# A 50-point transform in column halves of the TensorE array, with the work's order laid out anew

## The chip, the core and the metric

The kernel runs on one core of a Trainium2 chip. The metric is the device time of one launch in microseconds (us). The engines named below are TensorE (PE, with its weight loads shown apart as PEld), VectorE (DVE), ScalarE (ACT), GpSimd (POOL) and SyncE (SP), which here issues nearly all DMAs.

## What is computed

Eight sequences of 3200 positions with 256 channels go through a filter in the frequency domain and then a gated convolution. Cut to what matters:

```python
X = np.fft.rfft(x, axis=1)                      # x: (8, 3200, 256)
Yr = Xr @ w_r - Xi @ w_i + b_r                  # 256 x 256 weights
Yi = Xr @ w_i + Xi @ w_r + b_i
Y  = soft_threshold(Yr, 0.01) + 1j * soft_threshold(Yi, 0.01)
x  = np.fft.irfft(Y, n=3200, axis=1)

gate_pre = sum(conv_w[k] * shifted(x, k) for k in range(5))   # causal, per channel
out = (sigmoid(gate_pre) * (x @ w_val)) @ w_out
```

All of it is fp32 in and out.

## The kernel before

**The transforms.** 3200 is taken as 64 x 50 (N1 = 64, N2 = 50), so each transform is two short ones done as matrix products with constant matrices, once forth and once back. A batch (one of the eight sequences) goes through these steps, with the names of the trace:

- p1 (lines 553 to 560, tile p): the forward 50-point transform from x, 8 pieces a batch, on quarters of the array (64 x 64, with 50 rows used). The result is folded into s and stored to a_dram.
- s2 (line 631, tile s; line 623 for the last group): the forward 64-point transform on 64 x 64 quarters, 6 pairs of pieces and one whole-array piece a batch.
- mix_sum and mix (lines 749 and 745, tile y_ps; 735 and 736 for the last group): the products with the complex weights over the whole array. Operands are split into a high and a low part in the fp32r format, and three products of parts stand for one. The bias is seeded by line 727, the threshold is lines 757 and 759.
- s1i (line 700, tile z_ps; line 694 for the last group): the 64-point transform back, on 64 x 64 quarters. ACT copies it out (line 710), SP stores it to z_dram.
- s2i (line 810, tile y_p): the 50-point transform back. It is in `positions`, called 8 times a batch (k from 0 to 7). A z load (line 800) brings 100 rows (Q = 2 x 50) by 4 x 256 channels into zl. For each channel half c and each of 4 positions m, one fp32 product takes 100 rows by 128 channels of zl as weights and streams 100 columns of the constant g2; the result lies on 128 partitions, one per channel, and is copied by ACT to y_sb (line 814; for k = 0 lines 818 to 822).
- gated (lines 847 to 911): the value product v (line 844, tile v_ps), the convolution (lines 871 and 874, tile acc, on ACT and DVE), sigmoid (884), gate (886), the split of the gated values (348 and 350) and the projection o (line 844, tile o_ps). For the last batches v and o use unsplit fp32 weights (line 840, w_late). ACT copies o out (line 911) and SP stores it.

The forward part of one batch is interleaved with the back part of the batch before.

**What sets the order.** The order on every engine is fixed when the program is built, by the class `Plan`. `add(at, engine, busy, fn, ...)` gives a piece a due time `at`, an engine, an assumed duration `busy` in ns, what it uses and sets, and the buffers that it opens. `order` then simulates the engines: at each step it takes, among the pieces of one engine that could start within SLACK (20 ns; 50 on SP) of the earliest one, the piece with the lowest due time. The due unit is such that a batch has 13 (T = 13). The dictionary O holds the offsets of the due times ("load_z", "y", "conv" and so on), and two entries for PE's mode. The assumed durations are not those of the trace: s2i is planned at 1500 ns.

Each PE piece has a mode: "q" for pieces on quarters of the array, "f" for fp32 and "r" for fp32r on the whole array. SWITCH (line 239) adds about 100 ns for a passing into "q" or out of it, and nothing between "f" and "r". In the choice of the next piece (lines 191 to 193) a "q" piece gets its due time lowered by O["together"] while PE is in mode "q"; when PE is in another mode and only one "q" piece could start, its due time is raised by O["hold"]:

```python
lone = e == "PE" and sum(c[1]["mode"] == "q" for c in near) < 2
start, p = min(near, key=lambda c: (c[1]["at"] + (0.0 if e != "PE" or c[1]["mode"] != "q" else -O["together"] if mode == "q"
                                                   else O["hold"] if lone else 0.0), c[0]))
```

The buffers count too: SLOTS gives three buffers of two PSUM banks with the tag ps_2, which p1, s2, s1i, s2i, v and o share, two for y_ps, and three for zl.

Of the kernel before, what the change touches and what calls it, by code (L numbers as in the profile page):

```python
# [18 lines left out]
P = 128  # L19
HP = P // 2  # L20
# [4 lines left out]
Q = NH * N2  # L25
# [79 lines left out]
class Plan:  # L105
# [11 lines left out]
    def add(self, at, engine, busy, fn, uses=(), sets=(), new=None, delay=None, mode="r", kb=0, chain=None, extra=0):  # L117
        n = len(self.pieces)
        before = set()
        for key in uses:  # L120
            before |= set(self.writers.get(key, ()))
        for key in sets:
            before |= set(self.readers.get(key, ())) | set(self.writers.get(key, ()))
        for key in uses:
            self.readers.setdefault(key, []).append(n)
        for key in sets:
            self.writers[key], self.readers[key] = [n], []
        p = dict(n=n, at=at, engine=engine, busy=busy, fn=fn, before=before, new=new or {}, mode=mode, kb=kb, extra=extra,
                 tiles={key[:2] for key in (*uses, *sets)}, delay=busy + LAND[engine] if delay is None else delay)
        p["behind"] = {self.last[chain]} if chain in self.last else set()  # L130
        if chain:
            self.last[chain] = n
        self.pieces.append(p)
        return n

    def order(self):
# [41 lines left out]
        while len(done) < len(pieces):  # L178
            best = None
            for e in engines:  # L180
# [5 lines left out]
                if not could:  # L186
# [4 lines left out]
# [3 lines that stand above are left out]
                if best is None or start < best[0]:  # L194
# [56 lines left out]
def act(n, kind="copy"):  # L251
    return {"copy": 45, "cast": 95, "mul": 104, "conv": 187, "relu": 198, "sigmoid": 103}[kind] + n / 1.2
# [5 lines left out]
NW = (NT - 1) * N1 + P  # L258
NG = NT // 2 * P + P
T = float(NU)  # L260
O = {'spread': -31.571,
     'hold': 1.3548,
     'together': 0.9587,
     'later': 40.4566,
     'load_x': -3.5845,
     'p1': -4.4613,
     'p1_step': 1.7844,
     'load_a': -4.8762,
     's2': -1.2484,
     's1i': 0.7694,  # L270
     'p3': 3.4728,
     'load_z': -14.7609,
     'y': 13.0605,
     'conv': 13.0179,
     'val': 2.3373,
     'gate': -21.6564,
     'project': 4.8084,
     'late_val': 6.023,
     'late_out': 14.484,
     'turn': -25.2941,  # L280
     'pre': 0.9193,
     'mix_sum': -2.2347,
     'p1_1': -2.3762,
     'load_x_1': 3.5351,
     'p1_2': 0.8883,
     'p3_0': 0.312}
WARM = 2, 1, 1, 1, 8
SLOTS = {"x": 3, "zl": 3, "y_hl": 2, "s1": 2, "a": 2, "xs": 2, "sx": 1, "xz": 1, "tp": 3, "zst": 2,
         "acc": 2, "g_hl": 2, "o": 2, "ps_y": 2, "ps_2": 3, "a_dram": 2, "z_dram": 2}
# [6 lines left out]
def fourier_filter_then_gated_conv(ctx: ExitStack, tc: tile.TileContext, x, w_r, w_i, b_r, b_i,  # L296
                                   w_val, conv_w, w_out, f1, f2, g1, g2, out):
    nc = tc.nc
# [3 lines left out]
    dram = ctx.enter_context(tc.tile_pool(name="dram", bufs=2, space=bass.MemoryType.DRAM))  # L302
    LATE_VAL, LATE_OUT = set(LATE[int(O["late_val"]):]), set(LATE[int(O["late_out"]):])
    plan = Plan(SLOTS)
    add = plan.add
# [21 lines left out]
    def buffer(key, tag, shape, dtype=F32):  # L327
        pool = ps if tag.startswith("ps_") else dram if tag.endswith("_dram") else sb
        tl[key] = pool.tile(shape, dtype, name=key[0], tag=tag, bufs=SLOTS[tag])
        return tl[key]  # L330
# [7 lines left out]
    def two_banks(key, tag="ps_2"):  # L338
        return buffer(key, tag, [P, 2, 512])

    def split(at, n, key, src, high, low, uses=(), new=None, first=None):

        hl = key + ("high",), key + ("low",)

        def cast():
            if first:
                first()
            nc.scalar.copy(out=high(), in_=src())
        add(at, "ACT", act(n, "cast"), cast, uses, [hl[0]], new, chain=key[0])
        add(at + 0.001, "DVE", dve(n), lambda: nc.vector.tensor_tensor(out=low(), in0=src(), in1=f32(high()), op=ALU.subtract),  # L350
            [*uses, hl[0]], [hl[1]])
        return hl
# [26 lines left out]
    def from_float64(at, n, views, uses, done, new=None, first=None):  # L379
# [34 lines left out]
        for k, (fn, busy) in enumerate(steps):  # L414
            def piece(k=k, fn=fn):
                if k == 0 and first:
                    first()
                fn()
            add(at + O["later"] + O["spread"] * k, "DVE", busy, piece, uses, done, new if k == 0 else None, delay=busy + (130 if k == 12 else 0))

    def load_matrix64(at, name, w, dst, uses=()):
# [9 lines left out]
        def views():  # L431
# [4 lines left out]
                     lambda: [buffer(key, "zl", [P, MB * D]) for key in keys[1:]])  # L436
        split(at + O["later"] + O["spread"] * 13 + 0.02, n, ("w", name), lambda: tl[keys[1]][:, n:2 * n].rearrange("p (j d) -> p j d", j=2),
              lambda: dst[:, 0], lambda: dst[:, 1], [keys[1] + (0,)])
# [84 lines left out]
    def p1(b, u, at):  # L523
# [8 lines left out]
        def load(h):  # L532
            xt = room(kx, x_tag, 4 * D) if h in (0, None) else tl[kx]
            src = x[b].rearrange("(n m) c -> n (m c)", m=N1)
            for g in range(NH) if h is None else (h,):
                eng = QUEUES[g][1] if early else nc.sync
                lo = (N1 - 3 - 4 * u if g else 4 * u) * D
                n = 3 * D if g and u == 0 else 4 * D
                by_rows(eng, xt[half(g), 0:n], src[:, lo:lo + n], rows)
                if n < 4 * D:  # L540
                    by_rows(eng, xt[half(g), n:], src[:, NM * D:(NM + 1) * D], rows)
# [3 lines left out]
        else:  # L545
            add(at + O["load_x"] + O["load_x_1"] * (b == 1), "SP", 700, lambda: load(None), STORED if b == 1 else (),
                [kx + (0,), kx + (1,)], {kx: x_tag}, kb=400, chain="x")
# [245 lines left out]
    def positions(b, k, at):  # L793

        bk = (b, k)
        kz, kp = ("zl", bk), ("y_p", bk)

        def load():
            zt = buffer(kz, "zl", [P, MB * D])
            nc.sync.dma_start(out=zt[0:Q], in_=tl["z_dram", b][:, k * MB * D:(k + 1) * MB * D])  # L800
        add(at + O["load_z"], "SP", 400, load, [("z_dram", b, u) for u in range(NU)], [kz + (0,)], {kz: "zl"}, kb=400, chain="zl")

        def s2i():
            zt = tl[kz].rearrange("p (m c) -> p m c", m=MB)
            p = two_banks(kp)
            for c in range(2):
                for m in range(MB):
                    g = g2_sb[0:Q, 0:Q] if k == m == 0 else g2_sb[0:Q, Q:2 * Q]
                    dst = p[:, c, 0:TB].rearrange("p (g n) -> p g n", n=N2)[:, m:2 * MB - m:2 * MB - 1 - 2 * m, :]
                    nc.tensor.matmul(dst, zt[0:Q, m, c * P:(c + 1) * P], g, start=True, stop=True)  # L810
        add(at, "PE", 1500, s2i, [kz + (0,), ("g2", 0, 0)], [kp + (0,)], {kp: "ps_2"}, mode="f", chain="s2i")
        up = (H0 + MB * k) * N2
        if k:
            add(at + 0.1, "ACT", act(2 * TB), lambda: nc.scalar.copy(  # L814
                out=pair(y_sb, up, (N1 - MB + 1 - 2 * MB * k) * N2, MB * N2), in_=tl[kp][:, :, 0:TB].rearrange("p c (h n) -> p c h n", h=2)),
                [kp + (0,)], [("y", "up", k), ("y", "down", k)])
        else:
            add(at + 0.1, "ACT", act(TB), lambda: nc.scalar.copy(out=y_sb[:, :, up:up + MB * N2], in_=tl[kp][:, :, 0:MB * N2]),
                [kp + (0,)], [("y", "up", 0)])
            add(at + 0.1, "ACT", act(2 * (MB - 1) * N2), lambda: nc.scalar.copy(  # L820
                out=y_sb[:, :, (H0 + N1 - MB + 1) * N2:], in_=tl[kp][:, :, MB * N2:(2 * MB - 1) * N2]), [kp + (0,)], [("y", "down", 0)])
            add(at + 0.1, "ACT", act(2 * N2), lambda: nc.scalar.copy(out=mid_sb[:, b % 2], in_=tl[kp][:, :, (2 * MB - 1) * N2:TB]),
                [kp + (0,)], [("mid", b % 2, 0)])
        if k == 1:
            def turned():
                old = y_sb[:, :, N1 * N2:].rearrange("p c (m n) -> p c m n", n=N2)
                new = y_sb[:, :, 0:H0 * N2].rearrange("p c (m n) -> p c m n", n=N2)
                nc.vector.tensor_copy(out=new[:, :, :, 1:], in_=old[:, :, :, :N2 - 1])
            add(at + 0.1, "DVE", 283, turned, [("y", "down", 0), ("y", "down", 1)], [("y", "back", 0)])
        if k == NB - 1:  # L830
            mid = (H0 + NM) * N2
            add(at + 0.1, "ACT", act(2 * N2), lambda: nc.scalar.copy(out=y_sb[:, :, mid:mid + N2], in_=mid_sb[:, b % 2]),
                [("mid", b % 2, 0)], [("y", "mid", 0)])
# [138 lines left out]
    for b in range(B):  # L972
# [12 lines left out]
        start = (b + 1) * T + O["p3"] + O.get(f"p3_{b}", 0.0)  # L985
# [31 lines left out]
```

## Time and profile before

| | us |
|---|---|
| median of 3 runs | 877.88 (877.44 to 878.52) |
| the profiled execution | 876.76 |
| its span, first to last instruction | 875.0 |

The page gives the busy share of each engine over the span, then the chain of work that ended last, then groups of instructions by source line with their mean duration. A duration of one matmul in such a group runs from its start to its modelled end, and the matmuls overlap; so the time that a piece takes on PE is read from the distance of its start to the start of the next piece, in the chain in order of time. "x16" behind a line is the number of instructions merged there; an fp32 product is two instructions. In the table of windows each row is a stretch of the span with the busy time of PE, PEld, DVE, ACT and POOL, the clock that TensorE was granted, the DMA share and GB/s.

### The profile page before, as it was taken

The numbers are of one execution on the slowest core, as the hardware profiler recorded it, in microseconds if no ns is written. First come the engines' busy times: TensorE is split into PE (matmuls) and PEld (weight loads), VectorE is DVE, ScalarE is ACT, GpSimd is POOL, SyncE is SP. The second block draws the span as 40 slices with busy tenths as digits, with TensorE's granted clock in tenths as the row PEclk, the third lists the DMA queues.
The fourth block names the chain that finished last, engine by engine and source line by source line (L and its number), as shares of the span: only waits on it lengthen the run. The fifth ranks groups of instructions, "written<-read, shape, count | busy, mean of one in ns | idle before, by whom it ended". The sixth has DMA issues, their size and how long they took to land.

```text
span 875.0 us, 21750 instructions
## 1 busy us (share of the span) xinstructions
PE 841.8 (96%) x8790; PEld 726.1 (83%) x8790; DVE 767.1 (88%) x1262; ACT 617.9 (71%) x1030; POOL 3.7 (0%) x11
## 2 busy tenths in 40 slices
PE   8987987999999999999999999999999999999997
PEld 2355665988899989999999989989999999998874
DVE  2435598899999999999999999999999999899896
ACT  1323555787777786878878786878868787786663
POOL 0000000000000000000000000000010000000000
PEclk9967999999999999999999999999999999999999
DMA  6679777658774758747674767657674466415412
GB/s 169 184 186 234 222 197 230 220 175 257 224 214 153 222 158 247 235 149 204 216 239 146 224 173 253 217 157 210 212 216 136 133 166 179 123 64 168 150 60 92
DMA packets 123966, 162.13 MB, mean 185 GB/s; under 512 B 10592, under 2 KB 98298, under 8 KB 123866
## 3 DMA queue, kind: packets, MB, share of 16 engines
q1 hardware_dynamic: 122106, 157.47, 60.1%
q10 hardware_dynamic: 1760, 3.28, 1.4%
q8 instruction: 69, 1.13, 0.6%
q14 instruction: 31, 0.25, 0.1%
HBM read 82.06 MB, written 78.64 MB: 184 GB/s over the span
## 4 chain that ended last, share of the span: by engine, by line
PE 79%; DVE 9%; DMA 6%; ACT 3%; SPq 2%; issue 1%; ACTq 0%; DVEq 0%
PE o_ps L844 14%; PE y_ps L745 14%; PE v_ps L844 13%; PE y_p L810 13%; PE y_ps L749 7%; PE z_ps L700 5%; PE s L631 5%; PE p L553 4%; DMA x<-in_x 3%; DVE acc L874 3%; DMA a_dram<-s 2%; PE v_ps L840 2%; DVE st L390 1%; DVE acc L886 1%; PE y_ps L735 1%
## 5 line engine op out<-in xcount | busy, mean ns | idle before, releaser
L874 DVE SCALAR_TENSOR_TENSOR acc<-y_sb,cw_sb,acc 128x400 f32<-128x400 f32 x512 | 299.8, 626 | 4.7 <-ACT acc L871 3.5
L745 PE MATMUL y_ps<-w_sb,xs 128*128 128x256 f32 x1152 | 155.4, 284 | 3.7 <-DVE y_ps L751 3.6
L745 PEld LDWEIGHTS y_ps<-w_sb,xs 128*128 128x128 f32 x1152 | 143.9, 188 | 12.5 <-DVE y_ps L751 7.2
L844 PE MATMUL o_ps<-gated,wo_sb 128*128 128x400 f32 x744 | 151.3, 350 | 0.0
L844 PEld LDWEIGHTS o_ps<-gated,wo_sb 128*128 128x128 f32 x744 | 132.9, 188 | 6.6 <-DVE acc L886 3.2
L844 PE MATMUL v_ps<-y_hl,wv_sb 128*128 128x400 f32 x648 | 130.7, 347 | 0.3 <-ACT o L911 0.3
L572 DVE TENSOR_TENSOR s<-p,s 128x512 f32<-128x512 f32 (+2 forms) x144 | 89.6, 625 | 39.7 <-ACT s L568 22.1
L810 PE MATMUL y_p<-g_sb,zl 100*128 100x100 f32 x1024 | 123.7, 275 | 0.0
L810 PEld LDWEIGHTS y_p<-g_sb,zl 100*128 100x128 f32 x1024 | 121.5, 192 | 2.0 <-issue 0.4
L844 PEld LDWEIGHTS v_ps<-y_hl,wv_sb 128*128 128x128 f32 x648 | 114.7, 188 | 5.1 <-ACT y_ps L727 3.2
L749 PE MATMUL y_ps<-w_sb,xs 128*128 128x256 f32 x576 | 90.2, 296 | 8.9 <-ACT xs L683 4.1
L749 PEld LDWEIGHTS y_ps<-w_sb,xs 128*128 128x128 f32 x576 | 79.3, 196 | 17.2 <-ACT y_ps L727 4.8
L757 ACT ACTIVATE tp<-y_ps,nlam 128x512 f32<-128x512 f32 (+1 forms) x104 | 69.8, 673 | 22.0 <-PE y_ps L745 19.8
L871 ACT ACTIVATE acc<-y_sb,cw_sb 128x400 f32<-128x400 f32 x128 | 75.4, 625 | 9.6 <-DVE gated L350 8.9
L553 PE MATMUL p<-x,f_sb 50*64 50x512 f32 x256 | 75.6, 678 | 6.3 <-DMA x<-in_x 4.4
L759 DVE SCALAR_TENSOR_TENSOR tp<-y_ps,tp 128x512 f32<-128x512 f32 (+1 forms) x104 | 68.7, 662 | 10.0 <-ACT tp L757 9.6
L560 PE MATMUL p<-x,f_sb 50*64 50x512 f32 x240 | 76.5, 684 | 0.0
L631 PEld LDWEIGHTS s<-f_sb,a 64*64 64x64 f32 x3072 | 55.2, 139 | 21.1 <-issue 10.5
L884 ACT ACTIVATE acc<-acc 128x400 f32<-128x400 f32 x128 | 67.7, 540 | 6.1 <-DVE acc L874 5.9
L911 ACT COPY o<-o_ps 128x800 f32<-128x800 f32 x63 | 51.8, 822 | 26.6 <-PE o_ps L844 26.3
L814 ACT COPY y_sb<-y_p 128x800 f32<-128x800 f32 x56 | 46.3, 828 | 32.9 <-PE y_p L810 32.6
L886 DVE TENSOR_TENSOR acc<-v_ps,acc 128x800 f32<-128x800 f32 x64 | 62.9, 983 | 3.1 <-ACT acc L884 2.7
(84 smaller groups left out, 1008.7 us busy)
## 6 DMA issues: line engine op xcount, KB each, us to landing
zl<-z_dram SPq DMA_DIRECT2D x64, 400.0 KB
out<-o SPq DMA_DIRECT2D x126, 200.0 KB
a<-a_dram SPq DMA_DIRECT2D x96, 256.0 KB
z_dram<-z_t SPq DMA_DIRECT2D x48, 512.0 KB
x<-in_x SPq DMA_DIRECT2D x90, 200.0 KB
a_dram<-s SPq DMA_DIRECT2D x90, 200.0 KB
x<-in_x SPq DMA_DIRECT2D x23, 192.0 KB
a_dram<-s SPq DMA_DIRECT2D x15, 192.0 KB
```

The lines of the kernel that those rows point to most:

```text
L553: nc.tensor.matmul(p[k * HP:(k + 1) * HP, 0, :], f1_sb[half(0), 0:HP], xt[half(0), k * 512:(k + 1) * 512], start=True, stop=True)
L560: nc.tensor.matmul(dst, f1_sb[half(1), 0:HP], back[:, 2 * k:2 * k + 2, :], start=True, stop=True)
L572: nc.vector.tensor_tensor(out=st()[lo:hi, h, n], in0=tl[kp][lo:hi, 0, n], in1=st()[lo:hi, 1, n], op=(ALU.add, ALU.subtract)[h])
L631: nc.tensor.matmul(p[e * HP:(e + 1) * HP, h, c, t, :], tl[ka][rows, t, c * P + e * HP:c * P + (e + 1) * HP], f2_sb[rows, (4 * d + t) * N1: ...
L745: nc.tensor.matmul(p[:, 1 - r, :], xm(hx, c, r, i), w_sb[:, m, hw, c, :], start=False, stop=k == 5, skip_group_check=True)
L749: nc.tensor.matmul(tl[ky][:, 0], sm(hx, c, i), w_sb[:, 0, hw, c, :], start=False, stop=k == 5, skip_group_check=True)
L757: nc.scalar.activation(out=buffer(kt, "tp", [P, 2, D])[:, 0:n], in_=tl[ky][:, 0:n], func=AF.Relu, bias=nlam)
L810: nc.tensor.matmul(dst, zt[0:Q, m, c * P:(c + 1) * P], g, start=True, stop=True)
L844: nc.tensor.matmul(p[:, e, 0:TB], w[:, hw, c, e * P:(e + 1) * P], src(hy, c), start=n == 0, stop=n == 5)
L871: nc.scalar.mul(block(acc(c)), y_at(k, c, 0), cw_sb[:, c, 0:1])
L874: nc.vector.scalar_tensor_tensor(out=block(acc(c)), in0=y_at(k, c, j), scalar=cw_sb[:, c, j:j + 1], in1=block(acc(c)), op0=ALU.mult, op1=A ...
L886: add(at + O["gate"], "DVE", dve(2 * TB), lambda: nc.vector.tensor_tensor(out=tl[kg], in0=tl[kv][:, :, 0:TB], in1=tl[kg], op=ALU.mult), [k ...
```

## The change

The s2i product is issued in two halves of 64 channels (HP = 64), each writing to its own 64 partitions of the result, so that the one uses columns 0 to 63 of the array and the other columns 64 to 127. The planner's figure for the piece goes from 1500 to 1430 ns and its mode from "f" to "q". The due times and the two mode entries in O are other numbers; since they are inputs of the planner, the order of all engines' instructions may differ. Nothing else is changed: constants, loads, copies and buffers stay.

```diff
-O = {'spread': -31.571,
-     'hold': 1.3548,
-     'together': 0.9587,
-     'later': 40.4566,
-     'load_x': -3.5845,
-     'p1': -4.4613,
-     'p1_step': 1.7844,
-     'load_a': -4.8762,
-     's2': -1.2484,
-     's1i': 0.7694,
-     'p3': 3.4728,
-     'load_z': -14.7609,
-     'y': 13.0605,
-     'conv': 13.0179,
-     'val': 2.3373,
-     'gate': -21.6564,
-     'project': 4.8084,
+O = {'spread': -43.2582,
+     'hold': 0.1723,
+     'together': 1.3472,
+     'later': 16.9988,
+     'load_x': -1.6525,
+     'p1': -3.0866,
+     'p1_step': 1.6595,
+     'load_a': -5.4475,
+     's2': -2.5217,
+     's1i': 1.3927,
+     'p3': 3.8457,
+     'load_z': -27.5528,
+     'y': 14.5177,
+     'conv': 12.9924,
+     'val': 3.2379,
+     'gate': -21.5703,
+     'project': 5.6082,
      'late_val': 6.023,
      'late_out': 14.484,
-     'turn': -25.2941,
-     'pre': 0.9193,
-     'mix_sum': -2.2347,
-     'p1_1': -2.3762,
-     'load_x_1': 3.5351,
-     'p1_2': 0.8883,
-     'p3_0': 0.312}
+     'turn': -27.2503,
+     'pre': 6.946,
+     'mix_sum': -2.1531,
+     'p1_1': -2.5925,
+     'load_x_1': -0.3328,
+     'p1_2': 0.3179,
+     'p3_0': -1.1611}
...
                     dst = p[:, c, 0:TB].rearrange("p (g n) -> p g n", n=N2)[:, m:2 * MB - m:2 * MB - 1 - 2 * m, :]
-                    nc.tensor.matmul(dst, zt[0:Q, m, c * P:(c + 1) * P], g, start=True, stop=True)
-        add(at, "PE", 1500, s2i, [kz + (0,), ("g2", 0, 0)], [kp + (0,)], {kp: "ps_2"}, mode="f", chain="s2i")
+                    for e in range(2):
+                        nc.tensor.matmul(dst[e * HP:(e + 1) * HP], zt[0:Q, m, c * P + e * HP:c * P + (e + 1) * HP], g, start=True, stop=True)
+        add(at, "PE", 1430, s2i, [kz + (0,), ("g2", 0, 0)], [kp + (0,)], {kp: "ps_2"}, mode="q", chain="s2i")
```

## The prediction, made before the changed kernel ran

> **What bounds the kernel now.** I read the page first (shares of the engines, the chain that ended last), then the windows by stage, then the chain in order of time inside one batch.
>
> ```profile
> span 875.0 us, 21750 instructions
> ...
> PE 841.8 (96%) x8790; PEld 726.1 (83%) x8790; DVE 767.1 (88%) x1262; ACT 617.9 (71%) x1030; POOL 3.7 (0%) x11
> ...
> PE 79%; DVE 9%; DMA 6%; ACT 3%; SPq 2%; issue 1%; ACTq 0%; DVEq 0%
> ```
>
> PE holds 79% of the chain, but a busy PE is not a PE at its peak, and the stages differ. The windows separate them (columns: PE, PEld, DVE, ACT, POOL, granted clock, DMA):
>
> ```profile
> 0.00:110.00 110.00, 92.46 (x788) 51.84 (x789) 48.44 (x79) 37.16 (x64) 1.14 (x9) 0.86 0.77 198
> 110.00:207.00 97.00, 87.47 (x1047) 73.99 (x1046) 86.75 (x161) 67.39 (x116) 0.00 (x0) 0.98 0.69 210
> 207.00:790.00 583.00, 582.69 (x6545) 536.65 (x6544) 559.19 (x910) 461.78 (x769) 2.58 (x2) 1.00 0.62 189
> 790.00:840.00 50.00, 50.00 (x299) 43.08 (x299) 46.12 (x74) 33.90 (x56) 0.00 (x0) 1.00 0.44 140
> ```
>
> From 207 to 790 us PE idles 583 - 582.69 = 0.3 us at full granted clock. So there any PE time that really goes is span that goes, until DVE, idle for 583 - 559.19 = 23.8 us of the same stretch (4%), becomes the bound. Six batches lie in it, some 97 us each. The transform that the change touches, s2i (L810, tile y_p), is done there eight times a batch.
>
> Now the chain in order of time (start, us, line, count). With no idle on PE, a piece's time is the distance to the next piece:
>
> ```profile
> 500.73 0.45 PE s L623 x4
> ...
> 504.79 1.76 PE y_p L810 x16
> 506.55 1.09 PE s L631 x64
> 507.64 0.87 PE z_ps L700 x16
> 508.51 0.42 PE p L553 x2
> 508.93 0.01 PE p L560 x2
> 508.94 0.42 PE p L553 x2
> ...
> 514.59 0.43 PE z_ps L694 x2
> 515.02 1.42 PE y_ps L745 x12
> ...
> 528.04 1.94 PE y_p L810 x16
> 529.98 1.02 PE z_ps L700 x16
> ...
> 531.87 0.93 PE s L631 x64
> 532.80 1.96 PE y_p L810 x16
> 534.76 1.39 PE y_ps L745 x12
> ...
> 543.36 1.76 PE y_p L810 x16
> ...
> 547.00 0.93 PE s L631 x64
> 547.94 1.61 PE y_ps L745 x12
> 549.54 2.20 PE v_ps L844 x12
> ```
>
> Three things are to be seen. **First, s2i costs 1.76 us**, 16 instructions (each fp32 product is two), 110 ns each. L623 is also on the whole array with 128 weight columns, streams 128 columns where s2i streams 100, and takes the same 0.45/4 = 112 ns. L694, 256 columns, takes 0.43/2 = 215 ns. So streaming 100 columns should need 100/256 of 215, 84 ns, and what sets s2i's 110 ns is the loading of 128 weight columns.
>
> **Second, quarter-array pieces run four at once.** s (L631) is 64 instructions of 64x64 in 0.93 us, so 16 in a row in each quarter, 58 ns each. z (L700) is 16 in 0.87 us, 4 in a row, 217 ns each with 256 columns. p (L553, L560) with 512 columns takes 0.42 us a pass.
>
> **Third, passing between whole array and parts costs time.** s is 0.93 after p but 1.09 after s2i; z is 0.87 after s but 1.02 after s2i: 0.15 to 0.16 going in. Mix (y_ps) is 1.61 after s but 1.42 after a whole-array piece, and s2i is 1.96 after s but 1.76 otherwise: 0.19 to 0.20 coming out. Together 0.35 us for each run of part-array pieces.
>
> **The change part by part.** *The products.* 8 products become 16, half as wide in weights, in two column halves. The trace has no 128x64 tile. Bounds of one instruction: 58 ns (L631: 64 weight columns, but only 64 streamed) and 110 ns (L810 today). Between 64 columns at 58 ns and 256 at 217 ns lies 0.83 ns a column, so 100 columns give 58 + 36 x 0.83 = 88 ns; 64 weight columns load within the 58 ns. If the two halves run beside each other, as the column halves of L631, L700 and L553 must to give those times, s2i is 16 x 88 = **1.41 us, 0.35 less**. The ends: 16 x 58 = 0.93 (0.83 less) and 1.76 (nothing). I take 88 ns, because the stream of 100 columns cannot be shorter than L694's and L700's columns allow.
>
> The other engines get nothing new: one copy to y_sb still follows the last product, no DMA and no wait is added; PE gets 1024 more matmuls and as many loads. Issue does not bound it: L631 issues 64 pairs in 0.93 us, the new s2i 32 in 1.41.
>
> *The mode.* Before, s2i next to whole-array pieces paid no passing. Now an s2i alone between such pieces pays 0.15 + 0.20 = 0.35, all that it saves: **a lone s2i gains nothing**. One beside s, z or p pays nothing new and keeps its 0.35 (at first on the assumption that 128x64 and 64x64 count as one mode, as the planner's "q" has it). With all 64 beside others the saving would be 64 x 0.35 = 22.4 us; with all alone, 0.
>
> *How many are alone.* In today's order the eight of the batch from 458 to 553 us stand so: the four at 504.79, 528.04, 532.80 and 543.36 touch s or z; the four at 458.42, 469.74, 485.57 and 495.33 have y_ps behind and o_ps ahead.
>
> ```profile
> 456.23 2.20 PE o_ps L844 x12
> 458.42 1.76 PE y_p L810 x16
> 460.18 0.73 PE y_ps L749 x6
> ...
> 467.55 2.20 PE o_ps L844 x12
> 469.74 1.76 PE y_p L810 x16
> 471.50 0.73 PE y_ps L749 x6
> ...
> 485.57 1.89 PE y_p L810 x16
> 487.46 0.73 PE y_ps L749 x6
> ...
> 495.33 1.76 PE y_p L810 x16
> 497.10 1.44 PE y_ps L745 x12
> ```
>
> That is 4 x 0.35 = 1.4 us a batch, 8.4 in the six batches. Outside them, from 160 to 207 us and in the last 70, I count by the same rule some 3 more that keep it, 1 us. **Sum with today's neighbours: 9.4 us.**
>
> *The order laid out anew.* The planner now holds s2i as "q": while PE is in that mode, a ready "q" piece goes first if its due time is within "together" (0.96 before, 1.35 now, in units of a thirteenth of a batch, 7.5 us), and a single one is held back by "hold" (1.35 before, 0.17 now). Both counts can only move toward more neighbours, but three ps_2 buffers serve p, s, z, s2i, v and o, which caps a run. I take one s2i in two batches more than today, 4 x 0.35 = 1.4 us. The due times of load_z, spread, later, load_x_1, y and the rest move SP, DVE and ACT too. They choose only among pieces that the plan has ready within 20 ns (50 on SP), so a z load due 13 units earlier does not enter SP's queue before its stores are planned to be done. What they can win on PE is idle time: 9.5 us from 110 to 207 and 17.5 before; what they can lose has no cap but the waits. I take 0, with 3 us either way as an estimate of a third of those 9.5.
>
> *What is late next.* PE needs 1.4 to 1.6 us less of 97 a batch; DVE idles 23.8/6 = 4.0 us a batch, so it can follow, at 98% instead of 96%. Such tight DVE hands some waits back: I take off 1 us in all. Sum: 9.4 + 1.4 - 1 = 9.8 us. The profiled execution took 876.76 us (span 875.0 and 1.8 around it), so 867.0; the median of the three runs, 877.88, is 1.1 above it, so **868.0 us**.
>
> **The rivals.**
> 1. *128x64 and 64x64 are two modes.* Then each border between s2i and s, z or p costs what going in costs, 0.15 (a first load of 64 columns that nothing covers). A batch has four such borders, 0.6 of its 1.4 us; in all some 27 x 0.15 = 4 us: 872. For it: both known passings are changes of tile shape. Against: nothing in the trace shows this border. The Trainium skill, "TensorEngine Tiling (Array Packing)", Key Properties, says so outright: changing the tiling mode, not just the tile, drains the engine. By that rule the time is 872, without it 868; the rows for whole array against quarters agree with it, at 0.35 a pair.
> 2. *DVE or the copies keep the pace.* DVE has 4.0 us of slack a batch on average, but in order; if half of PE's saving turns into waits for buffers that DVE or ACT frees, 873 to 876. For it: DVE 96% busy; against: PE is to gain less than that slack.
> 3. *Slower: runs of part-array pieces wait for a ps_2 buffer.* The place: PE, ahead of the fourth piece of a run, while v, gate, mix and project queue behind it. The price: the copy of an earlier piece, which the next rows put at 0.83 to 1.01 us.
>
> ```profile
> L710 ACT COPY z_t<-z_ps 128x1024 f32<-128x1024 f32 x48 | 48.6, 1013 | 12.0 <-PE z_ps L700 10.9
> L814 ACT COPY y_sb<-y_p 128x800 f32<-128x800 f32 x56 | 46.3, 828 | 32.9 <-PE y_p L810 32.6
> ```
>
>  From about ten such waits the gain of 9.8 is gone; two a batch, 16, give 868 + 16 = 884. For it: the new order prefers long runs. Against: today a run of five (s2i, z, p, s, s2i, 528.04 to 534.76) shows no wait.
> 4. *The halves do not run beside each other with 100 rows.* Then s2i is 32 x 88 = 2.8 us, 1.05 more, 64 times: 945. Against: in every quarter-array row two column halves stream from the same partitions at once. The Trainium skill, "TensorE: Matmul & The Clock Gate", Part 3 (The mechanism), lets a weight load overlap a running matmul only when their row groups differ; both halves here have the same rows. The trace disagrees: v (L844) loads for 188 ns over all rows, yet a piece of 12 takes 2.20 us (549.54), 183 ns each, load and product.
>
> ```profile
> L844 PEld LDWEIGHTS v_ps<-y_hl,wv_sb 128*128 128x128 f32 x648 | 114.7, 188 | 5.1 <-ACT y_ps L727 3.2 <-ACT o L911 0.5 <-issue 0.4
> ```
>
> **How the numbers follow.** Forecast (862 to 871) 0.45; rival 1 (871 to 874) 0.21; rival 2 (873 to 877) 0.13; rival 3 (877 to 886) 0.13; rival 4 0.03; nearly all s2i with neighbours, 877.9 - 18 = 860 and below, 0.05. A measurement of this kernel tells about 0.2%, 1.8 us, from no change. Faster by more: 0.45 + 0.21 + 0.05 and two thirds of rival 2, 0.79. Within 0.2%: the rest of rival 2 and a bit of rival 3, 0.07. Slower: 0.14. The range runs from 861 to 878: it leaves out about 0.04 below and 0.14 above, and holds the crossings' cost from 0 to 0.15. The lower end of the product's price (0.93 us) would lie in the part left out below, the upper (1.76, no gain and 37 passings more, 13 us) above.
>
> **What would show it.** L810: twice the instructions, 64 columns of weights, 1.41 us from its first to its last start inside a run. After it, s, z or p at 0.93, 0.87, 0.85 us (forecast) or 0.15 more (rival 1). Runs of part-array pieces: about eleven a batch, some four lone s2i. PE still without idle from 207 to 790, DVE at 97 to 98%; PE waits for ACT L814 or L710 of about a microsecond mean rival 3, for DVE rival 2. The forecast is wrong if a lone s2i does not cost about 1.75 with its passings, if the new order leaves nearly all alone, or if the start before 207 us moves by more than 3 us.

## The result and the profile after

The changed kernel takes 867.45 us, the median of four runs (866.44 to 869.32), against 877.66 us (877.38 to 878.52) for the kernel before: a ratio of 0.9895, 95% interval 0.9875 to 0.9914, 10.2 us less. The prediction said 868.0. The number is right; the way to it is only partly so, and this section and the next show where two errors cancelled.

The profiled execution of the changed kernel is the slowest of its four, 869.32 us with a span of 867.5. Its page (the span, the busy time of the engines, the chain that ended last):

```profile
span 867.5 us, 23798 instructions
...
PE 825.7 (95%) x9814; PEld 696.1 (80%) x9814; DVE 768.2 (89%) x1262; ACT 612.6 (71%) x1030; POOL 6.2 (1%) x11
...
PE 61%; DVE 16%; DMA 11%; ACT 6%; issue 2%; SPq 2%; ACTq 0%; DVEq 0%
```

PE is busy 16.1 us less than before, and idle 41.8 us where it was idle 33.2. DVE does the same work. In the chain that ended last PE falls from 79% to 61%; DVE and DMA take its place. The windows of the changed kernel show where the new idle time is (columns as before):

```profile
0.00:207.00 207.00, 174.97 (x1983) 123.67 (x1984) 135.98 (x242) 106.59 (x182) 1.15 (x9) 0.88 0.75 206
207.00:790.00 583.00, 579.44 (x7339) 517.85 (x7338) 565.35 (x915) 459.35 (x773) 5.01 (x2) 1.00 0.63 190
```

Up to 207 us PE idles 32 us (27 before), at a granted clock of 0.88 (0.92 over the same stretch before). In the middle it now idles 3.6 us, where it idled 0.3; DVE has 17.7 us of slack left of 23.8. So PE still sets the pace there, but no longer without gaps.

The chain in order of time, in the same part of the kernel, shows the prices of the new pieces (start, us, line, count):

```profile
446.02 1.02 PE z_ps L700 x16
447.04 0.42 PE p L553 x2
447.46 0.01 PE p L560 x2
447.47 0.41 PE p L553 x2
447.89 0.01 PE p L560 x2
447.90 1.52 PE y_p L811 x32
449.43 1.09 PE s L631 x64
...
490.09 1.52 PE y_p L811 x32
491.62 1.02 PE z_ps L700 x16
...
504.25 1.02 PE z_ps L700 x16
505.28 0.97 PE s L631 x64
...
506.27 3.69 DMA a<-a_dram
509.95 1.20 DVE xs L680
...
526.79 2.90 PE y_p L811 x64
529.69 0.90 PE y_ps L749 x6
```

- s2i (now L811, 32 instructions) is 1.52 us after a whole-array piece (490.09, behind v) and equally 1.52 after p (447.90). Two in a row are 2.90 (526.79), so the second takes 1.38 and the first pays 0.14 for coming in: **about 1.37 us, 86 ns for each of 16 in a row, was 1.76**.
- s is 1.09 after s2i (449.43), and z is 1.02 (491.62). Both are what they cost after a whole-array piece, not the 0.93 and 0.87 of before after one another. **The border between the column halves and the quarters costs about 0.15 us, in each direction**, as much as coming in from the whole array.
- Going out to the whole array, y_ps (six products, 0.71 by itself) is 0.90 at 529.69: 0.19, as before.
- At 506 the chain leaves PE: it follows a load of a (DMA, 3.69 us) and then work of DVE. PE does not stand still meanwhile: from 504 to 514 us it runs other pieces and idles 0.25 us, just ahead of v at 513.64. So the smaller share of PE in the chain is not idle time of that size. In the chain of before from 440 to 560 us every step is PE's.

Where in the span the gain shows depends on what one follows. The last product of the forward part's last group (L623) comes 16 us earlier than before; the first of these rows is the kernel before, the second the changed one (count, shortest, median and longest ns, first and last start):

```profile
L623 PE MATMUL s<-f_sb,a x32: 271/275/298, 119.0 to 783.9; 128*128 128x128 f32 x32
```

```profile
L623 PE MATMUL s<-f_sb,a x32: 271/275/377, 106.3 to 767.9; 128*128 128x128 f32 x32
```

But 13 of these 16 us are already there at its first start. The gated steps (read at the DVE product with the gate, now L887, once in each of 64 steps) gain only 2 us over four batches: from the 9th to the 41st it is 388.2 us against 390.2. Here are the two rows of the changed kernel; those of the kernel before stand further down:

```profile
276.94 0.98 DVE L887 TENSOR_TENSOR acc<-v_ps,acc 128x800 f32<-128x800 f32 x1
665.18 0.98 DVE L887 TENSOR_TENSOR acc<-v_ps,acc 128x800 f32<-128x800 f32 x1
```

The 9th step itself comes 4 us later than before. Only from the 49th to the 57th step is there a large gain, 61.4 us for 70.1, more than the 7.5 us between the two spans. That fits an order which does forward work earlier and gated work no earlier, and so has less left to do beside the last gated steps. So the mere time of one kind of work says little about the total; the halves in the old order, below, show the gain batch by batch.

### The profile page after: what moved, and what is told of

Read it like the earlier page. It is cut to its first block, busy times and chain, and to the rows that moved or that the text cites. A ratio compares the mean times of both kernels' runs of the same rounds, so it can differ in the third digit from the quotient of the medians.

```text
span 867.5 us, 23798 instructions
## 1 busy us (share of the span) xinstructions
PE 825.7 (95%) x9814; PEld 696.1 (80%) x9814; DVE 768.2 (89%) x1262; ACT 612.6 (71%) x1030; POOL 6.2 (1%) x11
## 4 chain that ended last, share of the span: by engine, by line
PE 61%; DVE 16%; DMA 11%; ACT 6%; issue 2%; SPq 2%; ACTq 0%; DVEq 0%
PE o_ps L845 12%; PE y_ps L745 11%; PE v_ps L845 10%; PE y_p L811 8%; PE y_ps L749 6%; DVE acc L875 5%; PE z_ps L700 4%; PE s L631 4%; DMA x<-in_x 3%; PE p L553 3%; DMA a<-a_dram 3%; DMA a_dram<-s 3%; DVE s L572 2%; DMA f_sb<-in_f 1%; DVE tp L759 1%
## 5 line engine op out<-in xcount | busy, mean ns | idle before, releaser
L811 PEld LDWEIGHTS y_p<-g_sb,zl 100*64 100x64 f32 x2048 | 89.3, 137 | 26.0 <-issue 4.9
L811 PE MATMUL y_p<-g_sb,zl 100*64 100x100 f32 x2048 | 99.6, 252 | 0.5 <-issue 0.2
L872 ACT ACTIVATE acc<-y_sb,cw_sb 128x400 f32<-128x400 f32 x128 | 77.2, 630 | 12.0 <-DVE gated L350 11.9
L553 PE MATMUL p<-x,f_sb 50*64 50x512 f32 x256 | 71.2, 639 | 9.0 <-issue 6.3
L348 ACT CAST gated<-acc 128x800 fp32r<-128x800 f32 x62 | 53.4, 861 | 31.4 <-DVE acc L887 31.2
L560 PE MATMUL p<-x,f_sb 50*64 50x512 f32 x240 | 71.9, 646 | 0.0
L727 ACT COPY y_ps<-bias_sb 128x256 f32<-128x256 f32 x104 | 39.7, 382 | 45.5 <-DVE tp L759 38.5
L348 ACT CAST y_hl<-y_sb 128x800 fp32r<-128x800 f32 x54 | 46.5, 860 | 28.5 <-PE v_ps L845 26.5
L631 PEld LDWEIGHTS s<-f_sb,a 64*64 64x64 f32 x3072 | 52.1, 138 | 15.9 <-issue 6.8
```

The costliest lines, as they stand in the source:

```text
L553: nc.tensor.matmul(p[k * HP:(k + 1) * HP, 0, :], f1_sb[half(0), 0:HP], xt[half(0), k * 512:(k + 1) * 512], start=True, stop=True)
L560: nc.tensor.matmul(dst, f1_sb[half(1), 0:HP], back[:, 2 * k:2 * k + 2, :], start=True, stop=True)
L631: nc.tensor.matmul(p[e * HP:(e + 1) * HP, h, c, t, :], tl[ka][rows, t, c * P + e * HP:c * P + (e + 1) * HP], f2_sb[rows, (4 * d + t) * N1: ...
L811: nc.tensor.matmul(dst[e * HP:(e + 1) * HP], zt[0:Q, m, c * P + e * HP:c * P + (e + 1) * HP], g, start=True, stop=True)
L872: nc.scalar.mul(block(acc(c)), y_at(k, c, 0), cw_sb[:, c, 0:1])
```

## The experiments

Two counts carry the sums below, both taken along PE's order over the whole kernel: *runs* of part-array pieces (each pays about 0.35 us for in and out) and *borders* inside a run between s2i and s, z or p (about 0.15 each). Without s2i the order of before has 74 runs; with s2i in halves, 111 runs and 23 borders, because 37 runs are s2i alone. The changed kernel has 86 runs (9 of s2i alone) and 59 borders. The first expectations count some runs too many on both sides, since they take the last group's whole-array z for a quarter piece (80 for 74, 101 for 93); the differences are nearly the same.

### The halves without the order, and the order without the halves

The first kernel is the one before with the two inner lines of s2i alone changed; plan, due times and so the order stay. The second is the changed kernel with the one whole-array product put back, its order kept.

```diff
# halves_only: in the kernel before
-                    nc.tensor.matmul(dst, zt[0:Q, m, c * P:(c + 1) * P], g, start=True, stop=True)
+                    for e in range(2):
+                        nc.tensor.matmul(dst[e * HP:(e + 1) * HP], zt[0:Q, m, c * P + e * HP:c * P + (e + 1) * HP], g, start=True, stop=True)
# order_only: in the changed kernel, the reverse of it
```

> The order of before, with s2i issued in column halves. If the prices read from the changed kernel's chain hold (s2i 1.37 us for 1.76, 0.35 for each run of part-array pieces more, 0.15 for each border between s2i and s, z or p): 64 x 0.39 = 25.0 saved, 36 runs more (12.6) and 24 borders (3.6) given back, 8.8 us in all: 868.9, as long as PE sets the pace in the middle. If what the changed kernel gains comes from its order alone: within 1 us of 877.7. If a border costs nothing: 865.3.

> The order of the changed kernel, with s2i as whole-array products again. PE theory: 101 runs of part-array pieces in place of the 80 of before, 21 x 0.35 = 7.4 us more: 885. Order theory (the new order alone brings the forward work some 15 us ahead and the end with it): 867 to 872.

Measured: halves_only 866.33 us (865.41 to 869.68), ratio 0.9871 (0.9844 to 0.9899); order_only 884.93 us (883.95 to 886.74), ratio 1.0079 (1.0054 to 1.0103); the kernel before in the same runs 877.93. The total of halves_only lies nearer to the 865.3 of a free border than to 868.9; measured once more, below, it is 869.73. So the total does not decide on the border, and the rows of the chain do.

So **the halves alone give the gain (11.6 us here, 6.8 in the second measurement below), and the new order by itself costs 7 us**. PE's order has 93 runs for 74, 19 x 0.35 = 6.7 us. PE also idles more in order_only: 40.8 us over the span against 33.2, and from 207 to 780 us 573 - 570.06 = 2.9 us where it was 0.3.

```profile
207.00:780.00 573.00, 570.06 (x6395) 516.56 (x6394) 546.68 (x879) 445.13 (x743) 5.00 (x2) 1.00 0.63 189
```

So not all of the 7 need be passings, and that 6.7 comes so near it is partly luck. Most of it arises between the 9th and the 41st gated step: 396.8 us against 390.2, with 44 runs for 28 (16 x 0.35 = 5.6 us).

Where the halves gain is best seen here, since the order is that of before. The chain of halves_only in the same part as the rows of the prediction:

```profile
464.66 1.52 PE y_p L811 x32
466.18 0.91 PE y_ps L749 x6
...
499.43 1.52 PE y_p L811 x32
500.95 1.09 PE s L631 x64
502.04 0.87 PE z_ps L700 x16
```

The s2i alone at 464.66 and the y_ps behind it take 1.52 + 0.91 = 2.43; the same two took 1.76 + 0.73 = 2.49 before (469.74 and 471.50). **An s2i alone gains 0.06 us: next to nothing, as predicted.** With a neighbour (499.43) it takes 1.52 in place of 1.76 and s behind it stays at 1.09: 0.24 saved, 0.39 less one border. Matched piece by piece between the two traces from 207 to 790 us, the 25 lone pieces gain 0.07 us in the median, and the 11 single pieces with part-array work behind them 0.24.

The weight loads (PEld) at the same place show the border itself (in this view the time is that from the first start to the last end):

```profile
499.36 1.40 PEld L811 LDWEIGHTS y_p<-g_sb,zl 100*64 100x64 f32 x32 [0.26 <-DVE gated L350]
500.88 1.02 PEld L631 LDWEIGHTS s<-f_sb,a 64*64 64x64 f32 x64
501.81 0.65 PEld L700 LDWEIGHTS z_ps<-tp,g_sb 64*64 64x64 f32 x16
```

The last load of s2i ends at 500.76 and the first of s starts at 500.88, with 0.12 us between them in which no weights are loaded. From s to z, which have the same tile shape, the loads overlap: z's begin at 501.81, those of s run until 501.90. So at the change of shape the loads do not run ahead. What holds them back no run here tells.

The gain can be seen on DVE as well, which multiplies by the gate (L886, here L887) once in each of 64 steps. The first row of each pair is the 9th of them, the second the 41st, four batches later; first the kernel before, then halves_only:

```profile
272.69 0.98 DVE L886 TENSOR_TENSOR acc<-v_ps,acc 128x800 f32<-128x800 f32 x1
662.91 0.98 DVE L886 TENSOR_TENSOR acc<-v_ps,acc 128x800 f32<-128x800 f32 x1
```

```profile
269.77 0.98 DVE L887 TENSOR_TENSOR acc<-v_ps,acc 128x800 f32<-128x800 f32 x1
655.09 0.98 DVE L887 TENSOR_TENSOR acc<-v_ps,acc 128x800 f32<-128x800 f32 x1
```

390.2 us become 385.3: 1.2 us a batch, and 4 x 0.06 + 4 x 0.24 = 1.2 is also what the eight s2i of a batch give by the rows above.

### Does DVE set the pace?

One tap of the convolution is left out in three kernels (the output lacks the contribution of conv_w's third row), which takes 128 DVE instructions of 0.55 us away and leaves the order of all others.

```diff
         def tap(c, j):
+            if j == 2:
+                return
```

> The kernel before with the convolution's third tap left out (128 DVE instructions of 0.55 us, 8.7 us of DVE a batch). PE sets its pace from 207 to 790 us, so all theories expect only the end to shorten, where the chain runs over DVE: 2 x 0.55 us in each of the last five steps, 5.5 us: 872. Much below that, DVE or waits for it bind already before the change.

> The changed kernel with the same tap left out. If DVE keeps the pace in the middle of the changed kernel (step period 97.1 us a batch where PE's pieces add up to about 95.9): 1.2 us in each of six batches and 5.5 at the end come off, 867.5 - 12.7 = 855. If PE keeps the pace there, only the end: 862.

> Column halves in the order of before, with the convolution's third tap left out, as in the two kernels with less DVE work. If DVE does not bind in this order: 5.5 us off at the end, as in the kernel before (5.7), so 860.5. If with the shorter s2i DVE binds in the middle too: 1 us a batch more, 853.

Measured: 872.22 us for the kernel before without the tap (5.7 less than with it), 860.63 for the changed kernel (6.8 less than its 867.45, which is from other runs), 864.21 for the old order with halves (5.5 less than the 869.73 of halves_again beside it). The end alone was to give 5.5. So DVE does not set the pace in the old order, and **takes about 1 us from the changed kernel**, which the medians alone hardly separate. The trace helps: in the changed kernel without the tap PE idles 573 - 571.94 = 1.1 us from 207 to 780 us,

```profile
207.00:780.00 573.00, 571.94 (x7311) 512.55 (x7309) 514.11 (x809) 455.76 (x766) 3.85 (x2) 1.00 0.63 192
```

where it idles 573 - 569.44 = 3.6 us with it:

```profile
207.00:780.00 573.00, 569.44 (x7271) 508.56 (x7270) 555.81 (x899) 452.54 (x762) 5.01 (x2) 1.00 0.63 191
```

Of these gaps, 2.5 us go with the DVE work. But order_only idles 2.9 us in the same stretch with s2i at its old length, so most of them come with the new order and not with the shorter s2i. My expectation of 1.2 us in every batch was too high.

### Do the halves run beside each other because they take turns?

```diff
-            for c in range(2):
+            for c, e in ((c, e) for c in range(2) for e in range(2)):
                 for m in range(MB):
...
-                    for e in range(2):
+                    if True:
```

> The changed kernel with another order inside s2i: for each half of the channels first the four products of the lower columns, then the four of the upper, not the two column halves in turn. If the halves run beside each other whatever their order, 867. If a product starts only after the one issued before it has started, and one column half takes its products one after another, the four of each half take 8 x 86 ns in a row and s2i becomes up to 32 x 86 = 2.75 us, 1.38 more, 64 times: up to 955. That is the price of the prediction's fourth rival, brought about on purpose.

Measured: 893.53 us, one run, beside 878.68 for the kernel before. The chain shows the piece:

```profile
455.88 2.03 PE y_p L811 x32
457.91 1.09 PE s L631 x64
```

2.03 in place of 1.52, so 0.51 more, 64 times 33 us; 26 arrive in the total (893.53 against 867.45). Where two s2i follow each other, they take 3.63 us,

```profile
439.67 3.63 PE y_p L811 x64
```

so the second takes 1.60 (1.38 in the changed kernel), and loses only 0.22. When four products of one half are issued in a row, the halves run beside each other only in part, but better than one after another: s2i itself is 1.88 behind another piece and 1.60 behind its like, not 2.75. What lets them overlap in part was not tried. **Turns between the halves are worth 0.5 us for most pieces.**

### A planner that knows the border

The planner of the changed kernel has 0 for a border and 0.2 for a run; the trace says 0.15 and 0.35. Four kernels give s2i a mode of its own and the measured prices. priced_0 keeps the changed kernel's due times; in the three others a search over O, by the plan's own end, chose them.

```diff
-SWITCH = {"rq": 97, "fq": 97, "qr": 100, "qf": 100}
+SWITCH = {"rq": 155, "fq": 155, "qr": 190, "qf": 190, "rc": 150, "fc": 150, "cr": 190, "cf": 190, "qc": 150, "cq": 155}
...
-                lone = e == "PE" and sum(c[1]["mode"] == "q" for c in near) < 2
+                lone = e == "PE" and sum(c[1]["mode"] in "qc" for c in near) < 2
...
-        add(at, "PE", 1430, s2i, [kz + (0,), ("g2", 0, 0)], [kp + (0,)], {kp: "ps_2"}, mode="q", chain="s2i")
+        add(at, "PE", 1375, s2i, [kz + (0,), ("g2", 0, 0)], [kp + (0,)], {kp: "ps_2"}, mode="c", chain="s2i")
```

> The changed kernel's due times with the planner given the measured prices: 98 runs, 51 borders. By PE's prices 25.0 - 24 x 0.35 - 51 x 0.15 = 8.9 off: 869. If the prices in the planner were what the changed order lacks, whatever the due times: below 866.

> Column halves, the planner given the prices of the traces (s2i 1.375 us in a mode of its own, 0.15 into a part-array mode or between 128x64 and 64x64, 0.19 out to the whole array), and the due times searched anew for it. Its plan has 78 runs of part-array pieces (74 without s2i in the kernel before, 111 in the order of before with halves, 86 in the changed kernel) and 55 borders (23, 59). By PE's prices alone 25.0 - 4 x 0.35 - 55 x 0.15 = 15.3 us off 877.9: 862.6; the changed kernel by the same sum 25.0 - 12 x 0.35 - 59 x 0.15 = 12.0, of which it got 10.2. If borders cost nothing, or if waits and not PE's pieces decide, it is no better than 866.

> As priced_1, another set of due times: 91 runs, 52 borders. By PE's prices 25.0 - 17 x 0.35 - 52 x 0.15 = 11.3 off: 866.6. What lies between this and priced_1 beyond 4 us is idle time, not price.

> As priced_1, a third set of due times: 89 runs, 57 borders. By PE's prices 25.0 - 15 x 0.35 - 57 x 0.15 = 11.2 off: 866.7.

| | runs | borders | by PE's prices from 877.9, us | measured, us | PE idle 207 to 780, us |
|---|---|---|---|---|---|
| halves_only | 111 | 23 | 869 | 866.33 (again 869.73) | 0.8 |
| changed kernel | 86 | 59 | 866 | 867.45 (again 867.38) | 3.6 |
| priced_0 | 98 | 51 | 869 | 890.54 | 19.3 |
| priced_1 | 78 | 55 | 863 | 869.65 | 5.2 |
| priced_2 | 91 | 52 | 867 | 873.39 | 5.3 |
| priced_3 | 89 | 57 | 867 | 884.64 | 13.9 |

The measured prices did not help. The four priced orders take 7 to 22 us more than their prices say, and 5 to 19 us of that is idle time of PE in the middle, the last column. The middle of priced_0:

```profile
207.00:780.00 573.00, 553.66 (x6969) 487.47 (x6968) 538.20 (x860) 432.22 (x730) 2.90 (x2) 0.99 0.62 187
```

None of the four beats the changed kernel; priced_1, at a ratio of 0.9909, is not told from it (0.9895, and 0.9906 below). These orders came out of a plan alone; which waits the plan misses was not settled. Among the waits of priced_0 the largest on PE's side (us in total, times, longest) is

```profile
PEld y_ps L749 <- ACT y_ps L727: 22.1, 18, 3.0
```

the wait of mix_sum's weight loads for the bias seed that ACT copies into y_ps; in the changed kernel its total is half of that:

```profile
PEld y_ps L749 <- ACT y_ps L727: 11.3, 13, 3.1
```

### The order, measured once more

The changed kernel and halves_only, both unchanged, run once more side by side.

> The order of before with column halves once more, beside the changed kernel on one chip, to settle the 1 us between them. If the new order brings nothing beyond the halves: equal within 1 us, both some 11 us below the kernel before. If the halves alone are better: 865 to 866.5.

> The changed kernel beside it. By PE's prices its order should be 25.0 - 12 x 0.35 - 59 x 0.15 = 12.0 below the kernel before, the halves in the old order 25.0 - 37 x 0.35 - 23 x 0.15 = 8.6; if it is not below them by 3 us, idle time took that.

Measured: halves_again 869.73 us (868.17 to 871.79), ratio 0.9929 (0.9908 to 0.9950); after_again 867.38 (866.45 to 869.86), ratio 0.9906 (0.9887 to 0.9925); the kernel before 876.53. The first time halves_only was at 866.33, 1.1 below the changed kernel; now it is 2.4 above it, and its two intervals do not even touch. So a kernel's median can move by some 3 us from one set of runs to the next, more than the interval of one set says and more than the 1.8 us that the prediction allowed for. **The new order with halves is worth something between -1 and +2.4 us: not told from nothing**; the +2.4 comes from the one pair that ran side by side. By PE's prices it should have been worth 12 x 0.35 and 59 x 0.15 against 37 x 0.35 and 23 x 0.15, 3.4 us.

## Why the prediction was right, and where it was not

- **What bounds, and that s2i is set by its weight load: right.** With half the weight columns the piece falls from 1.76 to 1.37 us. I took 88 ns for one instruction; it is 86. 25.0 us in place of 22.4 over 64.
- **A lone s2i gains nothing: right.** 0.06 us instead of 0; 1.52 and then 0.19 for going out, 1.71 together, against the 1.75 that I gave.
- **"One beside s, z or p pays nothing new": wrong.** This is the step that failed, and it is the first rival: the border costs 0.15. The forecast gave it 0.21, against 0.45 for the free border. The rule of the Trainium skill ("TensorEngine Tiling (Array Packing)", Key Properties) that a change of the tiling mode, and not just of the tile, drains the engine was the better guide. The trace agrees that such a change costs time, with 0.93 against 1.09 for s and 0.87 against 1.02 for z; that it is a drain no run here shows.
- **"I take one s2i in two batches more than today": wrong in size.** I kept some four lone s2i a batch; the new order has 9 runs of s2i alone in the whole kernel. I read the two mode entries in O rightly as drawing s2i to its neighbours, and then trusted the three ps_2 buffers to prevent it; rival 3, a wait for them ahead of the fourth piece of a run, did not come: the run z, p, s2i, s from 446.02 to 450.52 shows no gap, and from 207 to 790 us PE waits 0.2 us in all for the copy y_sb and not at all for z_t, the two copies that this rival names.
- **These two cancel.** Mine: 9.4 + 1.4 = 10.8 us before waits. With the measured counts and my prices it would have been 64 x 0.35 - 12 x 0.35 = 18.2, so 7.4 more; the price of s2i adds 64 x 0.04 = 2.6; the 59 borders take 8.9. Sum 11.9, by luck near mine.
- **Waits: 1 us taken off; the sign is right, the size proves little.** 11.9 by prices, 10.2 measured. But in the profiled executions PE idles 8.6 us more (41.8 against 33.2): 5.0 of it before 207 us and 3.3 from 207 to 790. How that goes with a total only 1.7 us above the sum stays open. Of the 3.3 in the middle 2.5 go with less DVE work, yet order_only has nearly as much with the old s2i. So this is not rival 2, in which PE's saving turns into waits; the new order brings it.
- **The order, 1.4 us by neighbours and 0 with 3 either way by idle time: held as a sum** by the two pairs (-1 to +2.4). The parts were not: the neighbours should bring 3.4 by the measured prices, so idle time took 1 to 4.4 of it. The prediction also named a start that moves by more than 3 us before 207 us as a sign of being wrong, and the start did move: the first L623 by 13 us, PE's idle time there from 27 to 32, the 9th gated step by 4. That the same order costs 7 us without the halves was not foreseen, nor was it needed.
- **Rival 4** is excluded by the 1.37, and halves_in_turn shows how part of it can be brought about by the order of issue.

What was to be checked first, "s, z or p at 0.93, 0.87, 0.85 (forecast) or 0.15 more (rival 1)", told the two apart in the chain alone. The total alone would have passed the wrong account as right.

## What to carry to other kernels

When weight loads set the time of products with few streamed columns, as here with 110 ns for 100 columns, try halving the weight columns and running the two column halves beside each other, issued in turns; here that took the load off the path, with 86 ns. But count the changes of tile shape along the engine's order before and after. Each had a price here, 0.15 us between the two part-array shapes and 0.35 for in and out of the whole array. Price a piece by the distance between starts in the chain, alone and in each neighbourhood in which it occurs. Separate the rewrite from the new order with one kernel each: here the rewrite in the old order gave 11.6 us once and 6.8 the second time, the whole change 10.2 and 9.2, and the order alone cost 7.

## What was not expected

- A border between 128x64 and 64x64 tiles costs 0.14 to 0.16 us in either direction, the same as from the whole array into parts.
- The order in which the products of the two column halves are issued decides how far they overlap: 1.37 us in turns, 1.88 in fours (1.60 behind another s2i), while 32 x 86 ns would be 2.75.
- Four orders from a planner with the measured prices, whose own sums lie within 7 us of each other, spread over 21 us on the chip (869.65 to 890.54).
